# Values of two heads in a bank: head by head, or by turns tile by tile

## The chip, the cores and the metric

The kernel runs on one core of a Trainium2 chip. The metric is the device time of one execution in microseconds (us). Engines are called as in the profile: PE (TensorE, matmuls), PEld (its weight loads), DVE (VectorE), ACT (ScalarE), POOL (GpSimd), SP (SyncE, which issues the DMAs).

## What is computed

Attention with a window over 8 batches of 8 heads, 576 positions and 64 values per head, and behind it a two-layer network of 512 to 2048 to 512 with a bent activation, on all 4608 positions. All inputs are float32.

```python
mask_plain = (rel >= 0) & (rel < window)                                          # window = 32
mask_dil = (rel >= 0) & (rel < window * dilation) & (rel % dilation == 0)         # dilation = 4
masks = np.stack([mask_plain if h < H // 2 else mask_dil for h in range(H)], axis=0)
scores = np.where(masks[None, :, :, :], scale * np.matmul(q, k.transpose(0, 1, 3, 2)), -1000000000.0)
attn = np.exp(scores - np.max(scores, axis=-1, keepdims=True))
attn = attn / (np.sum(attn, axis=-1, keepdims=True) + 1e-09)
x = np.matmul(attn, v)                     # then heads side by side: x is 4608 x 512
...
h = x @ w_in
g = np.where(h >= 1, h, np.where(h <= -1, 0.0, (h + 1) ** 2 / 4.0))
out = g @ w_out
```

The last step of attention, `np.matmul(attn, v)`, is the part that the change touches.

## The kernel before

**Tiling.** The 576 positions of a head are cut into 6 tiles of 96 queries. A query sees only keys close to it, so a tile needs 128 keys. The dilated heads are sorted by position modulo 4 on the host, which makes their window a band as well. Two heads n and n+1 form a pair and share loads, and their outputs share the 128 partitions of a bank: the 64 values of head n in rows 0 to 63, those of head n+1 in rows 64 to 127.

**Attention of a pair.** `scores_pair` (L192, heads 0 to 15; its matmul is L207) or `scores_split` (L220, the other 48 heads; L230) puts scores into PSUM. `reduce` (L179, L181) adds the mask and finds the maxima on DVE. `softmax` (L282) or the steps of `pair` (L520) take the exponentials on ACT (L255, L297), sum (L298) and multiply by the reciprocals on POOL (L291, L280) or DVE (L277). The result c is transposed into tiles pt: by PE for heads 0 to 15 (`transpose_pe`, L324: L330 on PE, the copies L333 on ACT for tiles 0 to 3 and on DVE for tiles 4 and 5), by DVE for the rest (L306). Then `values` (L354) multiplies by v.

**The values of a pair.** `values(n)` fills two banks `o`, part 0 with the tiles 0 to 2 and part 1 with the tiles 3 to 5. In each bank it issues six matmuls (L365): the stationary operand is v (128 keys x 64 values), the moving operand pt (128 keys x 96 queries), both float32, and the output is 64 rows x 96 columns. Each such matmul leaves two LDWEIGHTS and two MATMUL records in the trace. Before the change the loop goes through the three tiles of head n and then through the three tiles of head n+1. Behind each part, `store_x` (L346) reads the bank, first on ACT (L349, xh) and then on DVE (L350, xl).

**The network.** x is kept as a rounded part xh and a rest xl, and likewise the weights and the activation, so each product takes three matmuls. `layer1` (L396, L403) needs 12 matmuls of 128 x 512 for a block of 128 hidden units and 512 positions, `layer2` (L431, L439) another 12. There are 9 x 16 = 144 such steps. The weights come as 64-bit numbers and are put together by `weights` (L108: L115 and L121 on ACT, L123 and L126 on DVE, L131 on ACT, L132 on POOL) in the first stage of the kernel.

**What sets the order.** The instructions of PE and SP are issued in the order in which the program is written (`manual_schedule`, L557). The other engines' orders are worked out at build time by a scheduler that simulates the program, so a change on PE can move theirs. `early_values` does the first four pairs (heads 0 to 7) ahead of the network; all later pairs are put into slots of the steps (`place`, L458): in the steady stage the values of a pair come once in 8 half steps of the loop over s, between a `layer1` and a `layer2`. Some matmuls with no use (`spin`, L160) keep PE running in the first stage.

Of the kernel before, what the change touches and what calls it, by code (L numbers as in the profile page):

```python
# [44 lines left out]
def body(ctx, tc, q, k, q2, k2, v, mask, eye, w_in, w_out, out):  # L45
# [275 lines left out]
    def pt_of(n):  # L321
        return first_pts[n] if n < len(first_pts) else pts[n % 2]
# [23 lines left out]
    def store_x(src, t, c, dst):  # L346
        xh, xl = xtile(t)
        with tc.high_priority(offset=60):
            last["act"] = nc.scalar.copy(out=dst(xh[:, c]), in_=src)  # L349
            last["dve"] = nc.vector.tensor_tensor(  # L350
                out=dst(xl[:, c]), in0=src, in1=dst(xh[:, c]).bitcast(F32), op=ALU.subtract
            )

    def values(n):  # L354

        b, h = divmod(n, H)
        plain = h < H // 2
        c, tok0 = h // 2, b * S

        end = TOK - tok0 % TOK  # L360
        for part in range(2):
            op = ps.tile([128, 512], F32, tag="att", name=f"o{n}_{part}", bufs=2)
            for j in range(2):
                for i in range(3):
                    PE.matmul(  # L365
                        out=op[64 * j : 64 * j + 64, i * QT : (i + 1) * QT],
                        lhsT=heads[n + j]["vt"][:, 3 * part + i],
                        rhs=pt_of(n + j)[:, 3 * part + i],
                        start=True,
                        stop=True,  # L370
                    )
            if plain:
                first = part * 3 * QT
                cuts = sorted({first, min(max(end, first), first + 3 * QT), first + 3 * QT})
                for a, z in zip(cuts, cuts[1:]):
                    t, at = divmod(tok0 + a, TOK)
                    store_x(op[:, a - first : z - first], t, c, lambda x: x[:, at : at + z - a])
            else:
                cuts = sorted({0, min(end // DIL, CLS), CLS})
                for a, z in zip(cuts, cuts[1:]):  # L380
                    t, at = divmod(tok0 + DIL * a, TOK)
                    store_x(
                        op[:, : 2 * CLS].rearrange("p (r i) -> p r i", r=2)[:, :, a:z],
                        t,
                        c,
                        lambda x: x[:, at : at + DIL * (z - a)].rearrange("p (i r) -> p r i", r=DIL)[
                            :, 2 * part : 2 * part + 2
                        ],
                    )
# [89 lines left out]
    def values_native(n):  # L479
        values(n)  # L480
        if n + 2 < native:
            load_values(n + 2)
# [8 lines left out]
    for n in range(native, nhead, 2):  # L491
        u = 27 + 4 * (n - native)
        for j, at in ((0, u), (1, u + 4)):
            place(at, lambda m=n + j: scores_split(m, 0))
            place(at + 1, lambda m=n + j: scores_split(m, 2))
            place(at + 2, lambda m=n + j: (scores_split(m, 4), after(m)))
        place(u + 4, lambda n=n: (transpose(n), load_values(n)))
        place(u + 8, lambda n=n: transpose(n + 1))
        place(u + 11, lambda n=n: values(n))
# [40 lines left out]
    def early_values(n):  # L540
        with tc.high_priority(offset=150):
            values(n)
# [145 lines left out]
```

## Time and profile before

| | us |
|---|---|
| median of 3 runs | 943.05 |
| lowest and highest | 942.95, 943.52 |
| the profiled execution's own time | 943.52 |
| its span in the trace | 941.7 |

The mean granted TensorE clock in the profiled execution is 0.994 of full speed. The page's slices of the span (1/40 of it, so 23.5 us each) show three stages: the first 57 us, in which the inputs and weights are loaded and the DMA engines are at their limit; then the network with the attention beside it up to 751 us; then the network alone. In the tables, "busy" is the time in which an instruction of that engine was under way. Rows of groups have the line, the engine, the operation, output<-inputs, the shape, the count, and then busy us and the mean ns of one. Rows of the timeline have the start, the length from the first start to the last end (us), and the instructions that follow one another without another kind between them, with their count; idle time before them and who ended it stand in brackets. Rows of a stage have its limits, its length, the busy us of PE, PEld, DVE, ACT and POOL with counts, and then the granted PE clock, the DMA share and GB/s. Rows of the chain of waits have the start, the length and the engine with its line.

### The profile page before, as it was taken

What the parts mean: (1) busy time and instruction counts of PE and PEld (TensorE: products, weight loads), DVE (VectorE), ACT (ScalarE), POOL (GpSimd) and SP (SyncE); (2) the same over time, 40 slices, a digit from 0 to 9 for tenths busy, and PEclk for the clock granted to TensorE, in tenths of its full rate; (3) what the DMA queues carried; (4) which work ended last, traced back from release to release, by engine and by line L of the source; (5) the groups of instructions that cost most, each with busy time, mean ns of one, the idle gap of its engine ahead of it and who ended that gap; (6) DMA issues with size and microseconds to landing.
All of it is one profiled execution on the core that took longest, in us unless ns stands there. A gap on an engine that the chain in (4) does not pass through costs nothing.

```text
span 941.7 us, 14427 instructions
## 1 busy us (share of the span) xinstructions
PE 924.8 (98%) x4886; PEld 753.1 (80%) x4886; DVE 685.0 (73%) x1982; ACT 486.9 (52%) x1336; POOL 239.8 (25%) x155
## 2 busy tenths in 40 slices
PE   7989989999999999999999999999999999999998
PEld 6777778888888888888888888888888888888886
DVE  6898877888887888878887888888877643334333
ACT  6778856555555556555555555555555322222222
POOL 4566543222222222222222222222222000000000
PEclk9989999999999999999999999999999999999999
DMA  9971002312232222122322213222321010001001
GB/s 348 406 293 45 1 26 63 106 58 69 69 114 69 69 66 89 57 68 69 114 69 69 64 58 105 69 69 70 113 70 42 2 45 1 1 1 46 0 1 46
DMA packets 31018, 73.87 MB, mean 78 GB/s; under 512 B 3520, under 2 KB 3808, under 8 KB 30944
## 3 DMA queue, kind: packets, MB, share of 16 engines
q1 hardware_dynamic: 30944, 72.94, 23.5%
q8 instruction: 39, 0.64, 0.3%
q14 instruction: 35, 0.29, 0.1%
HBM read 63.49 MB, written 9.44 MB: 77 GB/s over the span
## 4 chain that ended last, share of the span: by engine, by line
PE 89%; DMA 5%; DVE 3%; issue 1%; POOL 1%; ACT 0%; SPq 0%; DVEq 0%; POOLq 0%; ACTq 0%
PE acc L439 41%; PE h L403 40%; PE o L365 4%; PE s L230 4%; DMA wo_raw<-w_in 3%; DMA wi_raw<-w_in 1%; DVE wo_raw L123 1%; DMA vt<-v_in 1%; DVE wo_m L126 1%; DMA kr<-k_in 1%; DVE c L181 1%; POOL c L291 0%; PE t L330 0%; DVE wi_m L126 0%; DVE y L417 0%
## 5 line engine op out<-in xcount | busy, mean ns | idle before, releaser
L439 PE MATMUL acc<-wo,gh 128*128 128x512 f32 x1152 | 385.2, 396 | 0.0
L403 PE MATMUL h<-xh,wi 128*128 128x512 f32 x1152 | 362.3, 396 | 0.8 <-DVE gl L426 0.8
L439 PEld LDWEIGHTS acc<-wo,gh 128*128 128x128 f32 x1152 | 217.0, 188 | 48.4
L403 PEld LDWEIGHTS h<-xh,wi 128*128 128x128 f32 x1152 | 210.1, 189 | 42.8 <-DVE gl L426 1.0
L403 PE MATMUL h<-xl,wi 128*128 128x512 f32 x576 | 227.5, 395 | 0.0
L439 PE MATMUL acc<-wo,gl 128*128 128x512 f32 x576 | 225.6, 392 | 0.0
L143 POOL TENSOR_TENSOR kk<-kr,kk 128x608 fp32r<-128x608 f32 x48 | 94.8, 1976 | 422.3 <-ACT kk L139 422.3
L255 ACT ACTIVATE c<-c 96x128 f32<-96x128 f32 x330 | 129.0, 392 | 118.4 <-DVE c L181 118.4
L420 ACT ACTIVATE y<-y,consts 128x512 f32<-128x512 f32 x144 | 104.1, 723 | 124.9 <-DVE y L417 124.9
L423 ACT CAST gh<-h 128x512 fp32r<-128x512 f32 x144 | 84.4, 586 | 130.4 <-PE acc L439 128.2
L417 DVE TENSOR_SCALAR y<-h 128x512 f32<-128x512 f32 x144 | 99.2, 689 | 62.9 <-PE h L403 61.7
L422 DVE TENSOR_TENSOR h<-h,y 128x512 f32<-128x512 f32 x144 | 100.6, 698 | 49.6 <-ACT y L420 48.2
L403 PEld LDWEIGHTS h<-xl,wi 128*128 128x128 f32 x576 | 108.6, 188 | 25.3
L439 PEld LDWEIGHTS acc<-wo,gl 128*128 128x128 f32 x576 | 108.6, 188 | 21.3
L426 DVE TENSOR_TENSOR gl<-h,gh 128x512 fp32r<-128x512 f32 x144 | 98.5, 684 | 37.2 <-ACT gh L423 37.2
L306 DVE STREAM_TRANSPOSE pt<-c 32x192 f32<-32x192 f32 x288 | 106.0, 368 | 5.8
L249 DVE TENSOR_TENSOR c<-s,msk 96x256 f32<-96x256 f32 (+1 forms) x168 | 61.5, 377 | 39.7 <-PE s L230 38.7
L291 POOL TENSOR_TENSOR c<-c 96x768 f32<-96x768 f32 x56 | 83.0, 1483 | 17.0 <-DVE c L290 16.7
L181 DVE CUSTOM_DVE_ANT_0 c<-s,c 96x128 f32<-96x128 f32 x288 | 70.6, 280 | 1.0
L349 ACT CAST xh<-o 128x288 fp32r<-128x288 f32 (+8 forms) x112 | 38.3, 380 | 46.2 <-PE o L365 30.8
L255 ACT ACTIVATION_READ_ACCUMULATOR c<-c 96x1 f32 x330 | 62.1, 188 | 0.0
L230 PEld LDWEIGHTS s<-kk,qs 128*96 128x96 f32 x288 | 46.4, 161 | 15.7
(57 smaller groups left out, 660.6 us busy)
## 6 DMA issues: line engine op xcount, KB each, us to landing
kr<-k_in SPq DMA_DIRECT2D x56, 304.0 KB, 3.3
qr<-q_in SPq DMA_DIRECT2D x56, 288.0 KB, 2.8
vt<-v_in SPq DMA_DIRECT2D x32, 384.0 KB, 4.0
out<-out SPq DMA_DIRECT2D x36, 256.0 KB, 2.9
wi_raw<-w_in SPq DMA_DIRECT2D x16, 512.0 KB, 9.3
wo_raw<-w_in SPq DMA_DIRECT2D x16, 512.0 KB, 9.4
msk<-mask_in SPq DMA_DIRECT2D x1, 144.0 KB, 3.8
ident<-eye_in SPq DMA_DIRECT2D x1, 36.0 KB, 4.8
```

The source lines that it names most:

```text
L143: nc.gpsimd.tensor_tensor(out=kk[:, 1], in0=hd["kr"], in1=kk[:, 0].bitcast(F32), op=ALU.subtract)
L230: PE.matmul(out=sv[:, t - t0], lhsT=hd["qs"][:, t * QT : (t + 1) * QT], rhs=hd["ks"][:, :, t * QT : t * QT + 128], start=True, stop=True,)
L255: last["act"] = nc.scalar.activation(out=c[:, t], in_=c[:, t], func=AF.Exp, bias=st[:, 0, t : t + 1], scale=-1.0, accum_out=st[:, 1, t : t ...
L291: nc.gpsimd.tensor_tensor(out=c, in0=c, in1=spread(st[:, 2]), op=ALU.mult)
L306: nc.vector.transpose(out=pt[r : r + 32, :, 32 * g : 32 * g + 32], in_=c[32 * g : 32 * g + 32, :, r : r + 32],)
L403: PE.matmul(out=hp, lhsT=wi[f][:, w, 128 * c : 128 * c + 128], rhs=x[:, c], start=c == 0 and i == 0, stop=c == NC - 1 and i == len(terms) - 1,
L417: nc.vector.tensor_scalar(out=y, in0=hp, scalar1=-1.0, scalar2=1.0, op0=ALU.max, op1=ALU.min)
L420: nc.scalar.activation(out=y, in_=y, func=AF.Square, bias=half_t, scale=0.5)
L422: activated = nc.vector.tensor_tensor(out=hp, in0=hp, in1=y, op=ALU.max)
L423: copied = nc.scalar.copy(out=gh, in_=hp)
L426: nc.vector.tensor_tensor(out=gl, in0=hp, in1=gh.bitcast(F32), op=ALU.subtract)
L439: PE.matmul(out=acc[m], lhsT=g[:, r], rhs=wo[f][:, w], start=f == 0 and i == 0, stop=f == NF - 1 and i == len(terms) - 1,)
```

## The change

In `values`, the two inner loops change places: for each tile, first head n and then head n+1.

```diff
             op = ps.tile([128, 512], F32, tag="att", name=f"o{n}_{part}", bufs=2)
-            for j in range(2):
-                for i in range(3):
+            for i in range(3):
+                for j in range(2):
                     PE.matmul(
                         out=op[64 * j : 64 * j + 64, i * QT : (i + 1) * QT],
                         lhsT=heads[n + j]["vt"][:, 3 * part + i],
```

The same 384 matmuls are issued, in 32 blocks of 12. On PE nothing else moves. Here is a block of the steady kind, between a `layer1` (L403) and a `layer2` (L439); pt_67 and pt_68 are the transposed tiles of the two heads, o_0 and o_1 the two banks. Before:

```order
L403 MATMUL h_9_1254<-xl_368,wi_1061 128x512
L365 MATMUL o_0_1275<-pt_67,vt_1016 64x96 x3
L365 MATMUL o_0_1275<-pt_68,vt_1016 64x96 x3
L365 MATMUL o_1_1286<-pt_67,vt_1016 64x96 x3
L365 MATMUL o_1_1286<-pt_68,vt_1016 64x96 x3
L439 MATMUL acc_0_740<-wo_1130,gh_7_1154 128x512
```

And the first part of it in the change:

```order
L403 MATMUL h_9_1254<-xl_368,wi_1061 128x512
L365 MATMUL o_0_1275<-pt_67,vt_1016 64x96
L365 MATMUL o_0_1275<-pt_68,vt_1016 64x96
L365 MATMUL o_0_1275<-pt_67,vt_1016 64x96
L365 MATMUL o_0_1275<-pt_68,vt_1016 64x96
L365 MATMUL o_0_1275<-pt_67,vt_1016 64x96
L365 MATMUL o_0_1275<-pt_68,vt_1016 64x96
L365 MATMUL o_1_1286<-pt_67,vt_1016 64x96
L365 MATMUL o_1_1286<-pt_68,vt_1016 64x96
```

The first matmul of the second head moves from the fourth place of the block to the second.

DVE's order changes in the first 35 us, and by one place at three later ones. This is DVE in the first stage, around the transposes of heads 4 and 5 (t_4_440 and t_4_450 are their tiles 4 and 5 in PSUM, wi_m the weight words). Before:

```order
L277 TENSOR_TENSOR c_266<-c_266,sums 96x768
L333 COPY pts_xl<-t_4_440 128x192
L126 SCALAR_TENSOR_TENSOR wi_m_477<-wi_m_477,wi_raw_99 128x512
L333 COPY pts_xl<-t_4_450 128x192
L126 SCALAR_TENSOR_TENSOR wi_m_484<-wi_m_484,wi_raw_101 128x512
L333 COPY pt_67<-t_4_463 128x192
```

And in the change:

```order
L277 TENSOR_TENSOR c_266<-c_266,sums 96x768
L350 TENSOR_TENSOR xl_381<-o_1_413,xh_380 128x64
L126 SCALAR_TENSOR_TENSOR wi_m_477<-wi_m_477,wi_raw_99 128x512
L126 SCALAR_TENSOR_TENSOR wi_m_484<-wi_m_484,wi_raw_101 128x512
L333 COPY pts_xl<-t_4_440 128x192
L333 COPY pts_xl<-t_4_450 128x192
L333 COPY pt_67<-t_4_463 128x192
```

Both merges of weight words (L126) now stand ahead of the two copies. A little earlier, the sum of exponentials of head 6 (L298, c_264) moves ahead of the copy of head 3's tiles 4 and 5 (t_4_400).

ACT has the other copies of the same transposes (t_0_434 and t_0_444, tiles 0 to 3 of heads 4 and 5). Before:

```order
L121 ACTIVATE wi_raw_101<-wi_raw_101 128x512
L333 COPY pts_xl<-t_0_434 128x384
L333 COPY pts_xl<-t_0_444 128x384
L131 CAST wi_481<-wi_m_477 128x512
L333 COPY pt_67<-t_0_457 128x384
L131 CAST wi_488<-wi_m_484 128x512
```

And in the change:

```order
L121 ACTIVATE wi_raw_101<-wi_raw_101 128x512
L131 CAST wi_481<-wi_m_477 128x512
L333 COPY pts_xl<-t_0_434 128x384
L333 COPY pts_xl<-t_0_444 128x384
L131 CAST wi_488<-wi_m_484 128x512
L333 COPY pt_67<-t_0_457 128x384
```

Each of the two casts moves up, the first of them ahead of both copies. The orders of POOL and SP are the same in both kernels.

## The prediction

> **What bounds the kernel now.** I read the page's totals first, then the busy times by stage, then who waited for whom, then the single matmuls of one values block.
>
> ```profile
> PE 924.8 (98%) x4886; PEld 753.1 (80%) x4886; DVE 685.0 (73%) x1982; ACT 486.9 (52%) x1336; POOL 239.8 (25%) x155
> ```
>
> PE is busy 98% of the span. The average could hide stages of another kind, so here are three stages (time, then busy us of PE, PEld, DVE, ACT, POOL):
>
> ```profile
> 45.00:66.00 21.00, 18.44 (x106) 15.62 (x106) 20.97 (x36) 16.57 (x41) 14.32 (x11) 0.92 0.92 347
> 66.00:128.00 62.00, 59.44 (x341) 46.59 (x337) 54.92 (x124) 49.08 (x110) 36.15 (x27) 0.97 0.11 34
> 140.00:750.00 610.00, 610.00 (x3183) 497.22 (x3182) 494.72 (x1514) 336.94 (x1008) 163.39 (x96) 1.00 0.24 73
> ```
>
> From 140 to 750 us PE never stops, while DVE, the next one, works 494.72/610 = 81%. There the time is a plain sum of matmul times. From 45 to 66 us DVE is the full engine (20.97 of 21.00). After 60 us only two waits of PE are left in the whole list:
>
> ```profile
> PE t L330 <- POOL c L291: 2.4, 1, 2.4
> PE o L365 <- DVE pt L333: 1.8, 1, 1.8
> ```
>
> **The values block today.** Call head n "A" (rows 0 to 63 of the output bank) and head n+1 "B" (rows 64 to 127). A block has 12 matmuls, and each leaves two records (24). The first row below counts the blocks' records after 60 us: 672/24 = 28 blocks, the last near 751 us. The next two give the length of one block up to the next matmul.
>
> ```profile
> L365 PE MATMUL o<-pt,vt x672: 246/246/298, 65.4 to 751.7; 128*64 128x96 f32 x168
> 78.12 1.43 PE L365 MATMUL o<-pt,vt 128*64 128x96 f32 x24
> 79.48 0.50 PE L439 MATMUL acc<-wo,gh 128*128 128x512 f32 x1
> ```
>
> So 1.36 us for a block. How much of it already has A and B side by side is seen at 24.5 us, the one place where the two heads' tiles have different names (A is pts_xh, B is pts_xl; start, duration):
>
> ```profile
> 24.53 0.46 PE L365 MATMUL o<-pts_xl,vt 128*64 128x96 f32 x3 [0.48 <-ACT pts_xl L333]
> 24.75 0.30 PE L365 MATMUL o<-pts_xh,vt 128*64 128x96 f32 x1
> 24.83 0.25 PE L365 MATMUL o<-pts_xl,vt 128*64 128x96 f32 x1
> 24.88 0.25 PE L365 MATMUL o<-pts_xh,vt 128*64 128x96 f32 x1
> 24.91 0.25 PE L365 MATMUL o<-pts_xl,vt 128*64 128x96 f32 x1
> 24.97 0.25 PE L365 MATMUL o<-pts_xh,vt 128*64 128x96 f32 x1
> 24.99 0.25 PE L365 MATMUL o<-pts_xl,vt 128*64 128x96 f32 x1
> 25.05 0.25 PE L365 MATMUL o<-pts_xh,vt 128*64 128x96 f32 x1
> 25.07 0.25 PE L365 MATMUL o<-pts_xl,vt 128*64 128x96 f32 x1
> ```
>
> Each head alone starts a record every 82 or 83 ns (24.83, 24.91, 24.99, 25.07), whether or not the other runs: two streams, at full pace side by side. But the second stream joins late. The same in a block of the steady stage, through three windows from 173.30 to 173.50, 173.548 and 173.56 us, which show how many records had begun:
>
> ```profile
> 173.33 0.38 PE L365 MATMUL o<-pt,vt 128*64 128x96 f32 x2
> 173.33 0.46 PE L365 MATMUL o<-pt,vt 128*64 128x96 f32 x3
> 173.33 0.52 PE L365 MATMUL o<-pt,vt 128*64 128x96 f32 x4
> ```
>
> The second record starts at 0.38 − 0.246 = 0.134 us, the third at 0.46 − 0.246 = 0.214, and the fourth only 0.006 or so behind it: that is B's first, which has 0.298 in place of 0.246 (0.52 − 0.298 = 0.222). So A goes alone for 0.222 us. The block then follows as B's length: 0.222 + 0.134 (B's first step) + 10 × 0.0825 + 0.18 (from the last start, 78.12 + 1.43 − 0.246 = 79.30, to the next matmul at 79.48) = 1.361. That is the measured 1.36, so the model is complete.
>
> **What the change does to a block.** No instruction is added or removed. B's first matmul now stands second instead of fourth, behind one matmul of A (two records) instead of three (six). When it starts in that place is shown by the scores of the first heads (L207), which already take turns head by head; window 82.44 to 82.46 us:
>
> ```profile
> 82.45 0.35 PE L207 MATMUL s<-kr,qr 64*96 64x128 f32 x2
> ```
>
> Two records of different heads have both begun by 82.46, and the first of them at 82.45: the second head needs no more than 0.01 us, though the first head's second record is still to come. I take 0.006, the step at which B's first follows A's third today. The new block is 0.006 + 0.134 + 0.825 + 0.18 = **1.145 us**, 0.216 less. The bounds: if B waited until A's second record had begun, it would start at 0.134 + 0.006 = 0.140 and the gain would be 0.082; and nothing can make it larger than 0.222. I take 0.216, since the L207 row has the same two records for each matmul. What differs there is that the heads lie in different rows of the array, here in different columns; the rows at 24.5 us show that columns go side by side as well.
>
> 28 blocks × 0.216 = **6.0 us** off PE's time after 65 us.
>
> **Does the gain reach the end?** From 140 to 750 us PE waits for nothing. The chain of waits names what lies ahead of that:
>
> ```profile
> 65.37 1.43 PE o L365 x24
> 78.19 1.36 PE o L365 x24
> 105.37 1.36 PE o L365 x24
> 126.52 1.48 POOL c L291
> ```
>
> Three blocks come before the 2.4 us wait for POOL, which ends at 128 us; the other 25 count in full unless something comes late now. Two things could. The transposes that a block reads end far ahead, at 693.5 for the block at 700.99; and the bank that the next scores want is free when its DVE read ends, at 703.43 + 0.38 = 703.81, 1.4 us before they start at 705.20:
>
> ```profile
> L306 DVE STREAM_TRANSPOSE pt<-c x6: 367/369/372, 691.6 to 693.5; 32x192 f32<-32x192 f32 x6
> 703.43 0.38 DVE L350 TENSOR_TENSOR xl<-o,xh 128x224 fp32r<-128x224 f32 x1
> 705.20 0.40 PE L230 MATMUL s<-kk,qs 128*96 128x256 f32 x2
> ```
>
> Both slacks are above 0.216 us, and part 0 leaves PE earlier than before. DVE would be busy 494.72 of 610 − 25 × 0.216 = 604.6 us, 82%, so it stays behind PE. The chain passes through the three early blocks before it turns to DVE and POOL, so I let their gain through; if those two keep their own pace, 3 × 0.216 = 0.65 is lost.
>
> **Before 65 us.** Four more blocks run here, two of them cut up by waits for copies. DVE's and ACT's orders change a little: both weight merges (L126) now stand ahead of DVE's copies of t, and a cast (L131) ahead of ACT's copies.
>
> ```profile
> 28.69 0.36 DVE L333 COPY pts_xl<-t 128x192 f32<-128x192 f32 x1
> 28.97 0.68 DVE L126 SCALAR_TENSOR_TENSOR wi_m<-wi_m,wi_raw 128x512 uint32<-128x512 uint32 x1
> 29.58 0.82 ACT L333 COPY pts_xl<-t 128x384 f32<-128x384 f32 x2
> 30.30 0.61 ACT L131 CAST wi<-wi_m 128x512 fp32r<-128x512 f32 x1
> 30.17 1.18 PE L330 MATMUL t<-ident,c 96*128 96x96 f32 x12 [0.33 <-ACT pts_xl L333]
> 35.47 0.69 DVE L126 SCALAR_TENSOR_TENSOR wi_m<-wi_m,wi_raw 128x512 uint32<-128x512 uint32 x1 [0.92 <-ACT wi_raw L121]
> 43.01 9.17 DMA wo_raw<-w_in
> 52.20 0.54 DVE wo_raw L123
> ```
>
> The transposes at 30.17 wait for ACT's copies, which now come behind a 0.61 us cast: +0.6 for the blocks at 31 and 34 us, which give 2 × 0.216 = 0.43 back. ACT and DVE go on from there without a break worth the name into the full DVE stage, so about **+0.3 us** arrives at 65 us (0.2 by this sum, and some for the second block, whose copy waits behind a sum). Ends: −0.3, if the 0.92 us idle at 35.47 takes the delay and the blocks' gain stays (no less, because the weight that DVE takes up at 52.20 lands only at 43.01 + 9.17 = 52.18); +1.3, if the 0.61 and the 0.68 both come through with nothing given back.
>
> **The sum.** −6.0 + 0.3 = −5.7. The profiled execution took 943.52 us (span 941.7, and 1.8 around it), the median is 943.05, 0.05% apart; a difference in PE time is the same against both. 943.05 − 5.7 = **937.3 us**, 0.6% faster. About 0.2% (1.9 us) is what a measurement can tell from no change.
>
> **Rivals.**
> - *Paid back early* (0.09): the reordered DVE and ACT work costs 1.3 us at 65 us, and the blocks ahead of 128 us give nothing: 25 × 0.216 − 1.3 = 4.1, so 939.0. For it: DVE is full from 45 to 66 us. Against it: these stages have idle PE time and a transfer as a second bound.
> - *Half the overlap* (0.05): B starts behind A's second record, 28 × 0.082 − 0.3 = 2.0, so 941.0. Against it stands the L207 row.
> - *Much more* (0.01): today's matmuls start in program order after all, and overlap only at the three changes of head. A block would then last 20 × 0.0825 + 2 × 0.05 + 3 × 0.006 + 0.18 = 1.95 us, the change would bring 0.80 in each, 22.5 in all, and the time would be 920.9. Against it: the block lasts 1.36 us, and in the rows at 24.5 us three pts_xl of part 0 start behind the pts_xh of part 1 at 24.75, against the program's order.
> - *No change* (0.06): what is shortened comes back as PE's wait for DVE or a bank, 943. Against it: 81% and the two slacks.
> - *Slower* (0.06): A and B now load weights at the same instant. Today a load of A and one of B are 0.02 and 0.06 us apart in turn, as the matmuls at 24.97, 24.99 and 25.05 are. If two loads at once hold each other up, every pair pays the step that today only the first one pays, 0.134 in place of 0.0825: 0.006 + 11 × 0.134 + 0.18 = 1.66, and 28 × 0.30 = 8.4 us more, 951.5. It decides from a pair step of 0.0825 + 0.216/10 = 0.104 us on. Against it, two loads that overlap in time without any loss of pace (same place as above):
>
> ```profile
> 24.97 0.14 PEld L365 LDWEIGHTS o<-pts_xh,vt 128*64 128x64 f32 x1
> 24.99 0.14 PEld L365 LDWEIGHTS o<-pts_xl,vt 128*64 128x64 f32 x1
> ```
>
> The Trainium skill has rules that speak for the third and the last of these. Its page "TensorE: Matmul & The Clock Gate" says under "Part 3: Packing small matmuls — row/col tiling" that matmuls start and end strictly in program order; the row at 24.75 and those behind it disagree, so the rival of 920.9 hardly counts. The same part says that a weight load runs beside matmuls under way only where the row groups differ; A and B share all rows, so by that rule this change would go the way of the slower rival. These rows speak against the rule: the load at 24.99 begins while the other head's load and matmul of 24.97 are under way, and both heads' next steps are 82 ns all the same.
>
> **How the numbers follow.** One cost has no term yet: behind the wait that ends at 128 us the granted clock (third column from the end) is lower for a while.
>
> ```profile
> 128.00:140.00 12.00, 11.96 (x70) 9.74 (x71) 6.83 (x14) 5.41 (x12) 2.56 (x2) 0.86 0.00 1
> ```
>
> That is worth 12 × 0.14 = 1.7 us, and such a dip may shift or vanish. Chances: forecast 0.73, the rivals in their order 0.09, 0.05, 0.01, 0.06 and 0.06. The forecast by its terms reaches from 28 × 0.222 + 0.3 = 6.5 off (936.5) to 6.0 − 1.3 = 4.7 off (938.3). The low end goes on to 935.5 for a dip that vanishes (937.3 − 1.7 = 935.6), the high end to 939.6, which takes in the first rival with 0.6 beside it. The other four are left out, 0.18. Faster by over 0.2%: the forecast, the first and the third rival and most of the second, 0.87; same 0.07; slower 0.06.
>
> **What would show it.** In the changed profile a block should last 1.15 us, with two records in its first 20 ns and pairs every 82 or 83 ns; PE should still be without a wait from 140 to 750 us; and the block that now starts at 65.37 should start between 65.1 and 66.7. A block that stays near 1.28 means half the overlap; one above 1.36, loads that collide; a block of 1.15 with less than 4 us gained, that PE waits elsewhere, and the list of waits names where.

## The result and the profile after

The changed kernel takes 938.0 us (median of 4 runs, 935.99 to 938.79) against 943.0 (942.9 to 943.52). The ratio is 0.9941, with a 95% interval of 0.9927 to 0.9956: 5.0 us or 0.6% faster, where 5.7 were forecast. Two later sets of the same kernel gave 938.19 (ratio 0.9949, 0.9936 to 0.9961) and 938.13 (0.9946, 0.9932 to 0.9959).

The profiled execution of the changed kernel was the fastest one, 935.99 us with a span of 934.2; it is 7.5 us shorter than the one of before, which is more than the change is worth. The totals first:

```profile
PE 914.5 (98%) x4886; PEld 742.9 (80%) x4886; DVE 685.2 (73%) x1982; ACT 487.1 (52%) x1336; POOL 239.8 (26%) x155
```

The same number of instructions, and PE is still busy 98% of the span. PE's busy time fell by 10.3 us and the span by 7.5: PE stands still 2.8 us longer, half of it in a wait shown below that the profile of before doesn't have. DVE, ACT and POOL did the same work as before. The three stages from the prediction, and the one with the clock dip (limits, length, busy us of PE, PEld, DVE, ACT, POOL with counts, granted PE clock, DMA share, GB/s):

```profile
45.00:66.00 21.00, 18.42 (x106) 15.46 (x108) 20.97 (x36) 16.61 (x41) 14.35 (x11) 0.92 0.91 350
66.00:128.00 62.00, 58.01 (x348) 45.40 (x345) 55.52 (x125) 49.15 (x110) 36.18 (x27) 1.00 0.11 34
128.00:140.00 12.00, 12.00 (x78) 9.74 (x77) 7.82 (x20) 6.83 (x14) 2.58 (x2) 1.00 0.01 1
140.00:750.00 610.00, 610.00 (x3221) 496.06 (x3220) 496.82 (x1515) 338.26 (x1011) 163.38 (x96) 1.00 0.24 73
```

Four things are to be seen. From 140 to 750 us PE still has no gap, but 3221 instructions now begin or run there instead of 3183: the gain is real PE time. From 45 to 66 us nothing changed; DVE is as full as before. From 128 to 140 us the clock is 1.00 where it was 0.86: the dip did not occur in this execution. And from 66 to 128 us it is 1.00 where it was 0.97: a second dip, behind the wait at 65 us, is gone too. These are the two in the profile of before, asked for by themselves, each 3.41 us at half the clock:

```profile
66.82:70.23 3.41, 3.41 (x8) 2.66 (x9) 2.73 (x6) 3.15 (x7) 1.36 (x1) 0.50 0.41 115
128.26:131.67 3.41, 3.41 (x13) 2.83 (x12) 2.27 (x5) 1.62 (x3) 1.28 (x1) 0.50 0.00 0
```

The values blocks (count of records after 60 us, then one block and the matmul behind it, then the first 30 ns of another, from a window of 170.90 to 170.98 us):

```profile
L365 PE MATMUL o<-pt,vt x672: 246/246/298, 65.4 to 744.2; 128*64 128x96 f32 x168
78.12 1.21 PE L365 MATMUL o<-pt,vt 128*64 128x96 f32 x24
79.27 0.50 PE L439 MATMUL acc<-wo,gh 128*128 128x512 f32 x1
170.95 0.30 PE L365 MATMUL o<-pt,vt 128*64 128x96 f32 x2
```

A block now lasts 79.27 − 78.12 = 1.15 us (1.141 by the starts in ns), against 1.36. Two records are 0.30 us long together, where the first record of a head alone has 0.298: both heads begin within 0.01 us.

PE's waits from 60 us on; in the profile of before, there were only the first two:

```profile
PE t L330 <- POOL c L291: 2.4, 1, 2.4
PE o L365 <- DVE pt L333: 1.8, 1, 1.8
PE t L330 <- DVE xl L350: 1.4, 1, 1.4
```

The third one swallows the gain of the first block after 65 us, but the change did not make it. In the profile of before, PE came to these transposes later only because its clock was down from 66.82 to 70.23 us:

```profile
71.18 0.92 PE L330 MATMUL t<-ident,c 96*128 96x96 f32 x6
71.88 0.48 PE L439 MATMUL acc<-wo,gh 128*128 128x512 f32 x1
```

After, PE is not slowed, is there early and waits for the DVE reads of the values' bank:

```profile
71.75 0.36 PE L330 MATMUL t<-ident,c 96*128 96x96 f32 x2 [1.41 <-DVE xl L350]
71.89 0.48 PE L439 MATMUL acc<-wo,gh 128*128 128x512 f32 x1
```

The last DVE read there starts at 71.31 in both, so the network goes on at 71.88 and 71.89. The kernel before with the filled wait of experiment 3, whose clock did not dip here, waits just as long:

```profile
71.86 0.35 PE L330 MATMUL t<-ident,c 96*128 96x96 f32 x2 [1.42 <-DVE xl L350]
72.00 0.48 PE L439 MATMUL acc<-wo,gh 128*128 128x512 f32 x1
```

From the start of the block at 65 us (65.50 in that execution) to this L439 it is 6.50 us there, 6.51 in the profile of before and 6.48 after. DVE's reads set this time, so neither a shorter block nor a full clock brings anything here.

### The profile page after: what moved, and what is told of

Same layout as the page of the kernel before. It is cut to its first block, busy times and chain, and to the rows that moved or that the text cites. A ratio compares the mean times of both kernels' runs of the same rounds, so it can differ in the third digit from the quotient of the medians.

```text
span 934.2 us, 14426 instructions
## 1 busy us (share of the span) xinstructions
PE 914.5 (98%) x4886; PEld 742.9 (80%) x4886; DVE 685.2 (73%) x1982; ACT 487.1 (52%) x1336; POOL 239.8 (26%) x155
## 4 chain that ended last, share of the span: by engine, by line
PE 89%; DVE 6%; ACT 3%; issue 1%; POOL 1%; DMA 0%; DVEq 0%; POOLq 0%; ACTq 0%
PE acc L439 41%; PE h L403 40%; PE s L230 4%; PE o L365 3%; DVE c L181 1%; ACT c L255 1%; DVE wo_raw L123 1%; DVE wo_m L126 1%; DVE wi_m L126 1%; DVE c L298 1%; PE t L330 0%; POOL c L291 0%; PE s L164 0%; DVE xl L350 0%; DVE y L417 0%
## 5 line engine op out<-in xcount | busy, mean ns | idle before, releaser
L439 PE MATMUL acc<-wo,gh 128*128 128x512 f32 x1152 | 384.3, 395 | 0.0
L403 PE MATMUL h<-xh,wi 128*128 128x512 f32 x1152 | 361.0, 394 | 0.8 <-DVE gl L426 0.8
L439 PEld LDWEIGHTS acc<-wo,gh 128*128 128x128 f32 x1152 | 216.2, 188 | 48.3
L403 PEld LDWEIGHTS h<-xh,wi 128*128 128x128 f32 x1152 | 209.4, 188 | 42.6 <-DVE gl L426 1.0
L403 PE MATMUL h<-xl,wi 128*128 128x512 f32 x576 | 227.1, 394 | 0.0
L439 PE MATMUL acc<-wo,gl 128*128 128x512 f32 x576 | 224.9, 391 | 0.0
L403 PEld LDWEIGHTS h<-xl,wi 128*128 128x128 f32 x576 | 108.1, 188 | 25.2
L439 PEld LDWEIGHTS acc<-wo,gl 128*128 128x128 f32 x576 | 108.2, 188 | 21.1
```

The lines of the kernel that those rows point to most:

```text
L403: PE.matmul(out=hp, lhsT=wi[f][:, w, 128 * c : 128 * c + 128], rhs=x[:, c], start=c == 0 and i == 0, stop=c == NC - 1 and i == len(terms) - 1,
L439: PE.matmul(out=acc[m], lhsT=g[:, r], rhs=wo[f][:, w], start=f == 0 and i == 0, stop=f == NF - 1 and i == len(terms) - 1,)
```

## The experiments

Each run's edit is shown against the changed kernel; `order` holds (tile, head) pairs.

### 1. The changed kernel once more, and the two halves of the change

Three runs on one chip, next to the kernel before. First the changed kernel unaltered.

> The changed kernel unaltered, for its profile and its spread. Theory (late joining): a values block lasts 1.14 us instead of 1.36 in every steady block, so 27 blocks give 27 x 0.216 = 5.8 us, and 943.0 - 5.8 = 937.2 us. Rival (clock): the 7.5 us by which the first profile's span fell hold 1.7 us of a PE clock dip behind the wait at 128 us, which vanished there; where the dip is in the profile, the time should be near 938.5 to 939, and where it is gone near 936.

938.19 us (937.73 to 938.87), 1 us more than the theory's 937.2. The profiled execution took 937.73, between the theory's time and the rival's 938.5 to 939 for an execution with the dip. The dip is back in it:

```profile
127.73 1.22 PE L330 MATMUL t<-ident,c 96*128 96x96 f32 x6 [2.40 <-POOL c L291]
128.66 0.78 PE L439 MATMUL acc<-wo,gh 128*128 128x512 f32 x1
129.23 0.63 PE L439 MATMUL acc<-wo,gl 128*128 128x512 f32 x1
129.66 1.05 PE L439 MATMUL acc<-wo,gh 128*128 128x512 f32 x2
```

The 128x512 matmuls behind the wait last 0.63 us and start 0.43 apart, instead of 0.39 and 0.23. The same kernel has thus executions with and without the dip, and the profiled execution of 935.99 us was one without. Of the miss, 0.55 us are lost in the first stage, which the theory left out; the table below shows them.

Then turns for the late pairs only:

```diff
-            for i in range(3):
-                for j in range(2):
+            order = [(0, 0), (0, 1), (1, 0), (1, 1), (2, 0), (2, 1)] if n >= native else [(0, 0), (1, 0), (2, 0), (0, 1), (1, 1), (2, 1)]
+            for i, j in order:
```

> Turns for the 24 pairs from head 16 on alone; heads 0 to 15 as before, and so are DVE's and ACT's orders of the first stage. Theory: 24 blocks x 0.216 = 5.2 us, so 937.8 us, with the blocks at 65, 78, 105 and 136 us at 1.36 and the later ones at 1.14 us. Rival (early stage): if the first stage's new orders are what brings or costs time, this run differs from the changed kernel by 1 us or more beyond the 0.65 us of three blocks.

938.36 us, ratio 0.9951 (0.9939 to 0.9964), against a forecast of 937.8. Blocks of both kinds stand in its profile as expected: the first two rows are one of the early blocks, the last two one of the late ones.

```profile
77.97 1.43 PE L365 MATMUL o<-pt,vt 128*64 128x96 f32 x24
79.33 0.50 PE L439 MATMUL acc<-wo,gh 128*128 128x512 f32 x1
172.90 1.21 PE L365 MATMUL o<-pt,vt 128*64 128x96 f32 x24
174.04 0.50 PE L439 MATMUL acc<-wo,gh 128*128 128x512 f32 x1
```

And the reverse, turns for heads 0 to 15 only:

```diff
-            for i in range(3):
-                for j in range(2):
+            order = [(0, 0), (0, 1), (1, 0), (1, 1), (2, 0), (2, 1)] if n < native else [(0, 0), (1, 0), (2, 0), (0, 1), (1, 1), (2, 1)]
+            for i, j in order:
```

> Turns for heads 0 to 15 alone; the 24 later pairs as before. Theory: of the four blocks from 65 us on the first is swallowed by DVE, the other three give 0.65 us, so 942.4 us. Rival (clock): if a PE clock dip behind one of the waits vanishes or moves with the shift, 940.5 to 944.5 us, and the profile shows at which wait.

943.29 us (942.62 to 943.98, 11 runs), ratio 1.0002 (0.9993 to 1.0011), and not the 942.4 of the theory, which had left out the first stage. The early half of the change brings nothing that can be measured, and the late half brings all that can. Of the 0.65 us of three early blocks 0.55 are paid back in the first stage, as the next table shows. Everything in it is a start time read from the profiles: the first transposes of the kernel (L330), the values block near 65 us, the one near 136 us, and the span.

| profile of | first L330 | from there to the block at 65 | from the block at 105 to that at 136 | from the block at 136 to the end |
|---|---|---|---|---|
| before | 16.08 | 49.29 | 31.09 | 805.4 |
| changed, first profile | 15.57 | 49.84 | 29.19 | 800.0 |
| changed, second | 15.73 | 49.84 | 30.72 | 800.0 |
| late pairs only | 15.99 | 49.25 | 30.86 | 800.2 |
| early pairs only | 15.63 | 49.82 | 30.67 | 805.1 |

With turns in the early pairs, the way to the block at 65 us is 0.55 longer, every time. With turns in the late pairs, the last column is 5.2 to 5.4 shorter: 5.4 = 25 × 0.216 for 25 blocks, and 5.2 = 24 × 0.216 for 24. The column between holds the dip, where it occurs, and the gain of the block at 105 us. The first column holds the arrival of the inputs, which lies ahead of the first values and moves from one execution of the same kernel to another.

### 2. Does the turn matter, or the moment at which the second head joins?

One matmul of the second head is moved up, and the rest stays head by head.

```diff
-            for i in range(3):
-                for j in range(2):
+            order = [(0, 0), (0, 1), (1, 0), (2, 0), (1, 1), (2, 1)]
+            for i, j in order:
```

> In each bank A, B, A, A, B, B: only the first matmul of the second head is moved up, and the rest stays head by head. Theory (late joining): what counts is when the second head joins, so a block lasts 1.14 to 1.25 us and the time is 937 to 940 us. Rival (taking turns itself): only one of the three tiles takes turns, so a third of the gain: 1.29 us a block and 941 us.

939.55 us, ratio 0.9964 (0.9952 to 0.9977). A block:

```profile
77.90 1.26 PE L365 MATMUL o<-pt,vt 128*64 128x96 f32 x24
79.09 0.50 PE L439 MATMUL acc<-wo,gh 128*128 128x512 f32 x1
```

1.19 us, three quarters of the gain with one of three tiles taking turns: the moment of joining decides. The 0.05 us that remain are one step of the second head that takes 0.133 in place of 0.082, at its fourth record. It is as long as a head's first step. (In the steady stage the L439 matmuls behind each block take 0.035 us longer together than in the changed kernel, which costs this run almost another 0.9 us; why is not known.)

Then two matmuls of the first head ahead of the second:

```diff
-            for i in range(3):
-                for j in range(2):
+            order = [(0, 0), (1, 0), (0, 1), (1, 1), (2, 0), (2, 1)]
+            for i, j in order:
```

> In each bank A, A, B, B, A, B: two matmuls (four records) of the first head stand ahead of the second head's first. Theory (late joining, and it joins as soon as three records of the other head are left waiting): behind six records it joined with A's third, so behind four it joins with A's first or second, 0.01 to 0.14 us; a block lasts 1.15 to 1.28 us, 937.5 to 941 us. Rival (it joins a fixed 0.22 us late unless the heads alternate at once): 1.36 us a block, 943 us.

939.91 us, ratio 0.9964 (0.9950 to 0.9978). A block, and its start through a window of 78.80 to 78.84 us:

```profile
78.81 1.26 PE L365 MATMUL o<-pt,vt 128*64 128x96 f32 x24
80.00 0.50 PE L439 MATMUL acc<-wo,gh 128*128 128x512 f32 x1
78.81 0.31 PE L365 MATMUL o<-pt,vt 128*64 128x96 f32 x2
```

The second head joins 0.31 − 0.298 = 0.01 us after the first, over four records of it; again one step of the second head is long, at its eighth record, and the block has 1.19 us. The rival's fixed 0.22 us is out.

Last, the first head's six matmuls for both banks ahead of the second head's:

```diff
-        for part in range(2):
-            op = ps.tile([128, 512], F32, tag="att", name=f"o{n}_{part}", bufs=2)
-            for i in range(3):
-                for j in range(2):
+        ops = [ps.tile([128, 512], F32, tag="att", name=f"o{n}_{part}", bufs=2) for part in range(2)]
+        for j in range(2):
+            for part in range(2):
+                for i in range(3):
                     PE.matmul(
-                        out=op[64 * j : 64 * j + 64, i * QT : (i + 1) * QT],
+                        out=ops[part][64 * j : 64 * j + 64, i * QT : (i + 1) * QT],
...
+        for part, op in enumerate(ops):
```

> Head by head over both banks: six matmuls (twelve records) of the first head stand ahead of the second head's first. Theory: it joins with A's ninth record, 0.134 + 7 x 0.0825 = 0.71 us; a block lasts 0.71 + 0.134 + 0.825 + 0.18 = 1.85 us, 0.49 longer than before, so about 27 x 0.49 = 13 us slower than before, 956 us. Rival (the engine looks ahead far enough, and 0.22 us has another cause): 1.36 us a block, 943 us.

967.67 us, ratio 1.0259 (1.0245 to 1.0273), slower by more than forecast. The block is as forecast; here it is, and its records up to 78.975 and up to 78.995 us:

```profile
78.27 1.92 PE L364 MATMUL o<-pt,vt 128*64 128x96 f32 x24
80.12 0.50 PE L439 MATMUL acc<-wo,gh 128*128 128x512 f32 x1
78.27 0.87 PE L364 MATMUL o<-pt,vt 128*64 128x96 f32 x8
78.27 1.01 PE L364 MATMUL o<-pt,vt 128*64 128x96 f32 x10
```

1.85 us. Between the two windows two records begin, the ninth of the first head and the first of the second, 0.71 us into the block. The other 11 us were not forecast. PE now waits for DVE's reads of the banks, which both come free late; in the profile these waits are 8.5 of the 11 us:

```profile
PE s L230 <- DVE xl L350: 8.5, 11, 0.9
```

Together: with one, two, three and six matmuls of the first head ahead, the second joins after 0.006, 0.014, 0.222 and 0.71 us. In each case that is the moment at which three records of the first head, or fewer, are left unstarted ahead of it. Call the rows 0 to 63 and 64 to 127 of a bank, one for each head, its output halves. By these four points PE looks past three waiting records of the other output half, and not past more. All records here are of one shape, so whether the reach is a number of matmul records, of weight loads with them, or a time is open.

### 3. The clock dip

Eight matmuls without a use fill PE's wait for POOL; the edit to the changed kernel:

```diff
             tp = ps.tile([128, 512], F32, tag=tag, name=f"t{n}_{t0}", bufs=bufs)
+            if (n, t0) == (14, 0): spin(8, tp)
             for t in range(t0, t1):
```

> The changed kernel, with 8 matmuls of no use (16 records of 0.112 us, 1.8 us) in PE's 2.4 us wait for POOL ahead of the transposes at 128 us. Theory (clock): the granted clock falls in some executions because PE stands still there; with the wait filled no matmul behind it is slow, the stage from 128 to 140 us has a clock of 1.00, and the time is 0.5 to 1.5 us below that of the changed kernel, 937 us, with less spread. Rival (the dip has another cause): the slow matmuls stay, and the time is that of the changed kernel within 0.3 us.

> The changed kernel once more, as the measure for the run with the filled wait. Theory (clock): between 0 and 8 of the 128x512 matmuls behind the wait at 128 us start 0.2 us late each, another number than in its two profiles so far (none, 4); time 937.5 to 938.8 us.

936.75 us (ratio 0.9932, 0.9920 to 0.9945), against 938.13 for the changed kernel on the same chip: 1.4 us less, and the lowest median of all variants. The spread did not shrink with it as expected (1.2 us against 1.3). The wait, and the stage behind it:

```profile
125.71 1.95 PE L164 MATMUL t<-consts 128*128 128x128 f32 x16
128.28 0.71 PE L330 MATMUL t<-ident,c 96*128 96x96 f32 x6 [0.62 <-POOL c L291]
128.78 0.48 PE L439 MATMUL acc<-wo,gh 128*128 128x512 f32 x1
```

PE stands still for 0.62 in place of 2.4 us, and the matmuls behind it have their short form. The changed kernel beside it had the dip for the second time in its three profiles, with 7 slow matmuls and a clock of 0.86:

```profile
128.00:140.00 12.00, 11.66 (x70) 9.37 (x70) 6.93 (x14) 5.40 (x11) 2.86 (x3) 0.86 0.01 1
```

Is the dip a part of the change's account? The same fill in the kernel before, and once more in the changed one:

> The kernel before with the same 8 matmuls of no use in the wait at 128 us. Theory (clock): the dip behind that wait is as long with the old order of the values (5 slow matmuls in its profile), so this runs 0.7 to 1.5 us below the kernel before, 942.0 us, without a dip there. Rival (the change itself lengthens the dip and so gives back half a microsecond): the fill brings less than 0.6 us here, where it brought 1.4 us with the new order.

> The changed kernel with the filled wait, beside the kernel before with it. Theory: with the dip gone from both, what is left of the difference is 27 blocks x 0.216 - 0.3 for the first stage = 5.5 us. Rival: 5.0 us or less, the first figure of the change, and then the rest is lost elsewhere than in the dip.

941.82 us (ratio 0.9988, 0.9979 to 0.9997) and 937.19 us (0.9937, 0.9924 to 0.9951). The fill brings 1.2 us to the kernel before (0.3 to 2.0 by its interval), about as much as to the changed one, so there is no sign that the dip is a part of the difference. Neither profile has a slow matmul behind the wait. But the difference of 4.6 us is not the 5.5 of the theory; it is what the rival named. The two profiled executions, with spans of 940.2 and 935.4, show where the rest is in them: the first transposes start at 16.25 and 16.81 (0.56 lost in the arrival of the inputs, ahead of the first values), from there to the block at 65 us it takes 49.25 and 49.81 (0.56 lost in the first stage), and from that block to the end 874.7 and 868.8, 5.9 less, and 27 × 0.216 = 5.8. How early the inputs came in the executions without a profile is not known.

What decides whether an execution has the dip is not shown. Two things in the traces bear on it. Each of these stretches of low clock lasts 3.41 us, and its starts in one execution lie whole multiples of 3.41 us apart: 46.34, 66.82 and 128.26 us in the profile of before, 6 and 18 steps. And on this grid the wait lies elsewhere in each execution. Before, 2.4 us of it lie ahead of the step at 128.26; in the first profile of the changed kernel the step, at 45.06 + 24 × 3.413 = 126.98, falls into the wait and has 1.85 us of it ahead. The length of standing still ahead of the step is not all, since the run with six matmuls ahead had the dip behind 1.8 us. No run moved the wait on the grid.

## Why the prediction was right

**The block.** Forecast 1.145 us, measured 1.14 in all 25 blocks from 136 us on. The sum for today's block was right in its parts, too: its first term, 0.222 us in which one head goes alone, is what the change removes, and experiment 2 moved it at will.

**The rivals about the overlap.** "Half the overlap" would have shown 1.28 us, "slower" more than 1.36, "much more" a block of 1.95 us before the change; none did. Weight loads of both heads at the same instant cost nothing that shows. This is from the changed profile, where the records of both heads go on by steps of 0.08 us behind these loads (24.16, 24.24, 24.32 for the one, 24.16, 24.25, 24.33 for the other):

```profile
24.16 0.14 PEld L365 LDWEIGHTS o<-pts_xl,vt 128*64 128x64 f32 x1
24.16 0.14 PEld L365 LDWEIGHTS o<-pts_xh,vt 128*64 128x64 f32 x1
```

The block of 1.14 us is 12 steps in which two records run at a time. So the two rules of the Trainium skill that were weighed, matmuls strictly in the order of the program and weight loads beside matmuls only where the row groups differ ("TensorE: Matmul & The Clock Gate", "Part 3: Packing small matmuls — row/col tiling"), do not hold for the two output halves here.

**The reach to the end.** 25 blocks count in full, as forecast: 805.4 to 800.0 us from the block at 136 us on. PE's list of waits still has nothing there, so neither the bank nor DVE comes late.

**The count.** 28 blocks were forecast and 27 count. The step that failed is the one that let the gain of the block at 65 us through because the chain of waits passes through it: DVE's reads of its bank, which end near 71.6 us in both kernels, hold the next transposes. The chain ran through PE there only because the clock dip from 66.82 to 70.23 us hid this wait. That is 0.2 us.

**The first stage.** Forecast +0.3 us, measured +0.55 (49.84 against 49.29 in the table) to +0.57, and much the same in every profile with turns in the early pairs. The two mechanisms that were named both show, but in other sizes. The first is the cast that moved up and holds ACT's copies. In the changed kernel:

```profile
29.30 0.63 ACT L131 CAST wi<-wi_m 128x512 fp32r<-128x512 f32 x1
29.81 0.87 ACT L333 COPY pts_xl<-t 128x384 f32<-128x384 f32 x2
30.45 1.18 PE L330 MATMUL t<-ident,c 96*128 96x96 f32 x12 [0.79 <-ACT pts_xl L333]
```

The transposes wait 0.79 in place of 0.33 us, so the cast costs 0.46 and not 0.6. The second is the sum (L298) that DVE now does ahead of a bank's read and a copy that the second block, at 23 us, needs. Before, and then in the changed kernel:

```profile
24.20 0.21 DVE L350 TENSOR_TENSOR xl<-o,xh 128x64 fp32r<-128x64 f32 x1
24.34 0.34 DVE L333 COPY pts_xl<-t 128x192 f32<-128x192 f32 x1
28.00 1.15 PE L330 MATMUL t<-ident,c 96*128 96x96 f32 x12
23.61 0.94 DVE L298 TENSOR_REDUCE c<-c 96x6 f32<-96x768 f32 x1
24.47 0.21 DVE L350 TENSOR_TENSOR xl<-o,xh 128x64 fp32r<-128x64 f32 x1
24.60 0.34 DVE L333 COPY pts_xl<-t 128x192 f32<-128x192 f32 x1
27.81 1.15 PE L330 MATMUL t<-ident,c 96*128 96x96 f32 x12
```

Measured from the first transposes, the ones behind that block come 0.32 us late (27.81 − 15.57 against 28.00 − 16.08), ahead of the cast; this is the part that the forecast put at 0.1 and called "some". With the 0.46 the block at 31 us is 0.79 late (31.56 − 15.57 against 31.28 − 16.08), and the one at 34 us 0.57. Of the two blocks' gain only the first came through; some 0.55 then stays to 65 us. The term was too small by 0.27.

That the loss comes from the new orders and not from the turns is seen in two runs of experiment 2. The one with one matmul moved up has DVE's and ACT's orders of the kernel before at these places, and reaches the block at 65 us 49.12 us after its first transposes, 0.17 earlier than before. The one with two by two has the changed kernel's, and takes 49.86.

**The dip.** It was put at 1.7 us and only into the range. It is worth 1.5 us (30.72 against 29.22 us between two blocks, the second of these with the filled wait) to 1.6 (31.09 against 29.45 in the kernel before), and it comes or goes from one execution to the next. Without it, and without the 0.5 us by which its inputs came earlier, the first profile's 7.5 us are 5.4.

**The sum.** 27 × 0.216 − 0.57 = 5.3 us, against 5.0, 5.0 and 5.2 measured in three sets. The two terms that were off erred the same way, so no luck of one against the other is in the sum. What is left, 0.1 to 0.3, is within the intervals (1.2 to 1.4 us to either side) and within what the arrival of the inputs moves (15.57 to 16.81 us in these profiles).

## What to carry to other kernels

In these runs, two matmuls that write different halves of a bank's rows ran side by side only once both were within PE's reach: write such matmuls so that the halves alternate (1.14 us a block), or at least so that the second half's first matmul stands second or third (1.19, against 1.36 in fourth place). The worth of such a change is the stretch that the first half runs alone, times the blocks on PE's path, and not the length of what is reordered. Where a scheduler orders the other engines, look at what it moves in stages that PE doesn't bound; here it cost a tenth of the gain. And compare stages between fixed marks before a profiled execution is believed: this one held 2 us of clock and early inputs that the change had not earned, and the one of before hid a wait behind a dip of the clock.

## What the runs showed of the hardware

The first three are for float32 matmuls of 128 x 64 weights by 128 x 96, two records each.

- A second output half joins when three records of the first, or fewer, are still waiting: 0.006, 0.014, 0.222 and 0.71 us for one, two, three and six matmuls ahead.
- Records of the two halves start out of the program's order. Each half alone keeps its order and its 82 ns.
- Where the second half's matmuls did not alternate with the first's from the start, one of its steps took 0.05 us more, which made a block 1.19 instead of 1.14 us. That it comes into reach too late is a reading, and not tested by itself.
- In nine profiles PE's wait for POOL, 1.8 to 2.4 us long, was left as it is: in eight 4 to 8 matmuls at half pace followed, in one none. With the wait cut to 0.62 or 0.64 us there were none in three profiles.
- The granted clock in these dips is 0.50 for 3.41 us, and the dips of one execution start multiples of 3.41 us apart.
